# A new order for the first part of a one-core kernel: gated convolution, attention and channel mixing in one program

## The chip, the core and the metric

One core of a Trainium2 chip runs the whole program. The metric is the device time of one execution in microseconds (us), the median over runs. TensorE (PE) multiplies matrices; PEld is its weight load, which overlaps the multiplication. VectorE (DVE), ScalarE (ACT) and GpSimd (POOL) do elementwise work, and SyncE (SP) issues transfers. A row with a q behind the engine's name (SPq, ACTq) is a transfer being issued by that engine's queue.

## The reference

```python
kv = np.einsum('bhsd,bhse->bhde', k, v)            # q, k, v: (8, 8, 576, 64)
out = np.einsum('bhsd,bhde->bhse', q, kv)
out = out / np.sqrt(np.mean(out*out, -1, keepdims=True) + 1e-6) * g_norm
x = out.transpose(0, 2, 1, 3).reshape(8, 576, 512)

h = np.maximum(x @ w_in, 0.0)                      # w_in (512, 1024)
conv = sum(conv_w[j] * shift(h, j - 1) for j in range(3))   # along the sequence
x = (h / (1 + np.exp(-conv))) @ w_out              # w_out (1024, 512)

xn = (x - mean) / np.sqrt(var + 1e-6) * g_ln
out = x + np.maximum(xn @ w_ch1, 0.0) @ w_ch2      # (512, 2048), (2048, 512)
```

`shift` stands for the zero-padded copy of h moved by one row. The arithmetic is float32 (weights arrive as 64-bit numbers).

## The kernel before, in words

The 4608 rows of all batches are 36 tiles of 128 rows; three tiles make a chunk of 384 columns. The kernel is a list of small steps, each a Python function with arguments, and each has a place (a number, its slot). The list is sorted by place and written out in that order. Every engine runs its instructions strictly in the order in which they were written, and waits on semaphores for what it needs from the others. So the sorted list is the schedule: a step that waits holds up all later steps of its engine.

Names of steps, as they stand in the order (`b` a batch, `t` a tile of 128 rows, `f` one of 8 slices of w_in or w_out, `i` = 8 x chunk + f):

- `load_kvh_b_j`, `load_kvr_b`: k and v of a batch (two halves of 2 x 512 KB and a remainder of 2 x 128 KB); `load_q_t` (256 KB, tiles 0 to 3), `load_q2_u`: q of tiles 2u and 2u+1 in 16 or 32 small transfers; `load_w_winf`, `load_w_woutf` (512 KB each); `load_w_w10` is the first slice for the last part of the program. All transfers take one of 8 semaphores in turn, so the ninth waits for the first to land.
- Weights: `round_w0` (ACT, two instructions, L206 and L207), `cv_vec` (DVE, L213 and L214) and `cv_pool` (POOL, L221) turn the 64-bit number into float32. Then `split_win0`/`split_w0` (ACT, L248/L237) make the high half, `split_win1`/`split_w1` (DVE L253, or L242 on DVE or POOL) the low half, since each product is three passes of high and low halves.
- Attention: `kv_pair` (PE, L312), `kv_evac` (DVE, L319); `tq` and `tq_evac` (PE L360, ACT L365) transpose q for tiles 0 to 3, `tq_blocks` (DVE, L353) for later ones; `qkv` (PE, L377); `st_a`, `st_v`, `st_p` (ACT, DVE, POOL: the root mean square), `x_norm` (DVE, L404), `tx_first` (PE, L420), `xe_a`, `xe_l`, `xe_h` (ACT, DVE, POOL: the transposed tile and its low half, and the neighbours' columns).
- Convolution: `gemm1_i` (PE, L495, 12 matmuls into `h`), `conv_a` (ACT, L520), `conv_t` (first tap: L514 on DVE, L511 on ACT), `conv_v` (two taps on DVE, L535), `gate_a`, `gate_v` (ACT L546, DVE L552), `gsplit_a`, `gsplit_l` (ACT L556; low half L561 on POOL or DVE), `gemm2_c_f` (PE, L570, 9 matmuls into `accA`), `y_evac`, `y_store`.

The first chunk's `gemm1_0` needs tiles 0 to 3 and the first weight slice. Steps of the last part (names `w1`, `w2`, L580 and up) begin to mix in at slot 25.

Three tuples say which steps go to which engine: `TAP_VEC` (first taps on DVE), `LO_POOL` (low halves of w_out on POOL), `G_POOL` (low halves of the gate on POOL). The table `MOVED` gives single steps another place than the loops gave them:

```python
plan = [(slot + n * 1e-4, fn, args) for slot, evs in events.items() for n, (fn, args) in enumerate(evs)]
plan = [(MOVED.get(label(fn, args), pos), fn, args) for pos, fn, args in plan]
with tc.manual_schedule():
    for _, fn, args in sorted(plan, key=lambda e: e[0]):
        fn(*args)
```

Of the kernel before, what the change touches and what calls it, by code (L numbers as in the profile page):

```python
# [27 lines left out]

MOVED = {
# [28 lines left out]
G_POOL = tuple(range(21))  # L60


@with_exitstack
def tile_kernel(
# [949 lines left out]
    for c in range(CB):  # L1014
# [75 lines left out]
    def label(fn, args):  # L1090
        keys = ["".join(map(str, a)) if isinstance(a, tuple) else str(a) for a in args if isinstance(a, (int, str, tuple))]
        return "_".join([fn.__name__, *keys])

    plan = [(slot + n * 1e-4, fn, args) for slot, evs in events.items() for n, (fn, args) in enumerate(evs)]
    plan = [(MOVED.get(label(fn, args), pos), fn, args) for pos, fn, args in plan]
    with tc.manual_schedule():
        for _, fn, args in sorted(plan, key=lambda e: e[0]):
            fn(*args)
# [24 lines left out]
```

## Time and profile before

| | us |
|---|---|
| median of 3 runs | 1326.61 (1326.54 to 1329.29) |
| the profiled execution, its own time | 1328.66 |
| its span, first to last instruction | 1326.9 |
| PE busy in the span | 1274.0 (96%) |
| DVE, ACT, POOL busy | 910.1, 548.8, 284.8 |

PE is busy for 96% of the span, so what can be had lies in the 4% in which it is not, and in the stretches in which its clock is granted at less than full speed (a mean granted clock of 0.985). Busy shares over the whole span hide that the first 170 us look quite different from the rest; the rows below are therefore by stretch.

### The profile page before, as it was taken

What the parts mean: (1) busy time and instruction counts of PE and PEld (TensorE: products, weight loads), DVE (VectorE), ACT (ScalarE), POOL (GpSimd) and SP (SyncE); (2) the same over time, 40 slices, a digit from 0 to 9 for tenths busy, and PEclk for the clock granted to TensorE, in tenths of its full rate; (3) what the DMA queues carried; (4) which work ended last, traced back from release to release, by engine and by line L of the source; (5) the groups of instructions that cost most, each with busy time, mean ns of one, the idle gap of its engine ahead of it and who ended that gap; (6) DMA issues with size and microseconds to landing.
All of it is one profiled execution on the core that took longest, in us unless ns stands there. A gap on an engine that the chain in (4) does not pass through costs nothing.

```text
span 1326.9 us, 19380 instructions
## 1 busy us (share of the span) xinstructions
PE 1274.0 (96%) x6949; PEld 1136.9 (86%) x6949; DVE 910.1 (69%) x1752; ACT 548.8 (41%) x1063; POOL 284.8 (21%) x303
## 2 busy tenths in 40 slices
PE   6779999999999999999999999999999999999998
PEld 6668788989898989788888999899998999989997
DVE  3998787878888887777767666667666666673223
ACT  2664465556565566644442223222322322232221
POOL 2584443323333231133310000100000000100000
PEclk8799999999999999999999999999999999999999
DMA  9555267336552331487767674866576576656561
GB/s 279 137 139 126 67 183 200 112 82 187 157 152 73 100 116 45 154 283 254 259 243 293 193 244 151 300 207 208 192 271 203 176 277 231 209 205 258 174 222 48
DMA packets 184052, 245.90 MB, mean 185 GB/s; under 512 B 92668, under 2 KB 121364, under 8 KB 183956
## 3 DMA queue, kind: packets, MB, share of 16 engines
q1 hardware_dynamic: 182032, 243.59, 57.2%
q10 hardware_dynamic: 1924, 1.07, 0.3%
q8 instruction: 55, 0.90, 0.3%
q14 instruction: 41, 0.34, 0.1%
HBM read 202.66 MB, written 41.94 MB: 184 GB/s over the span
## 4 chain that ended last, share of the span: by engine, by line
PE 60%; DVE 17%; ACT 7%; SPq 6%; DMA 5%; issue 3%; POOL 1%; DVEq 0%; ACTq 0%; POOLq 0%
PE accB L814 27%; PE u L736 14%; PE v L736 7%; DVE a L535 5%; SPq L344 4%; PE accA L570 4%; PE h L495 4%; PE c L736 4%; DVE a L552 2%; DVE zx L428 2%; DMA raw_w<-in_moe_w_ch 2%; DMA raw_win<-in_moe_w_in 1%; ACT a L511 1%; ACT a L546 1%; ACT g L556 1%
## 5 line engine op out<-in xcount | busy, mean ns | idle before, releaser
L814 PE MATMUL accB<-w2s,r 128*128 128x512 f32 x1440 | 376.1, 393 | 0.0
L814 PEld LDWEIGHTS accB<-w2s,r 128*128 128x128 f32 x1440 | 267.3, 188 | 38.5
L736 PE MATMUL u<-z,w1s 128*128 128x384 f32 x1152 | 236.5, 340 | 8.2 <-DVE r L796 5.6
L495 PE MATMUL h<-xt,win 128*128 128x386 f32 (+1 forms) x1152 | 227.1, 346 | 6.6 <-ACT hs L520 3.4
L570 PE MATMUL accA<-wout,g 128*128 128x512 f32 x864 | 223.3, 402 | 8.4 <-DVE wout L242 2.6
L736 PEld LDWEIGHTS u<-z,w1s 128*128 128x128 f32 x1152 | 207.8, 189 | 27.4 <-DVE r L796 8.5
L495 PEld LDWEIGHTS h<-xt,win 128*128 128x128 f32 x1152 | 206.0, 191 | 15.8 <-ACT hs L520 4.8
L570 PEld LDWEIGHTS accA<-wout,g 128*128 128x128 f32 x864 | 160.2, 191 | 41.2 <-DVE wout L242 2.9
L791 ACT ACTIVATE r<-t 128x384 fp32r<-128x384 f32 x144 | 75.7, 526 | 261.6 <-DVE t L784 261.6
L778 ACT COPY u<-u 128x384 f32<-128x384 f32 x144 | 68.7, 477 | 218.5 <-PE u L736 218.5
L535 DVE SCALAR_TENSOR_TENSOR a<-hs,cols,a 128x384 f32<-128x384 f32 x192 | 138.9, 724 | 27.0 <-ACT a L511 23.1
L428 DVE STREAM_TRANSPOSE zx<-xc 32x128 f32<-32x128 f32 x480 | 145.3, 303 | 7.4
L796 DVE SCALAR_TENSOR_TENSOR r<-t,r 128x384 fp32r<-128x384 f32 x144 | 80.4, 559 | 85.2 <-ACT r L791 85.2
L679 POOL TENSOR_SCALAR mv<-mv 128x1 f32<-128x1 f32 x36 | 25.0, 694 | 478.8 <-DVE mv L670 470.9
L736 PE MATMUL v<-z,w1s 128*128 128x384 f32 x576 | 116.8, 337 | 0.0
L736 PEld LDWEIGHTS v<-z,w1s 128*128 128x128 f32 x576 | 103.6, 188 | 8.1
L784 DVE TENSOR_TENSOR t<-v,u 128x384 f32<-128x384 f32 x96 | 53.4, 556 | 73.7 <-ACT u L778 55.5
L546 ACT ACTIVATE a<-a 128x384 f32<-128x384 f32 x96 | 50.4, 525 | 116.0 <-DVE a L535 116.0
L400 POOL TENSOR_TENSOR r<-ss,mhalf 128x8 f32<-128x8 f32 x36 | 66.6, 1850 | 79.0 <-DVE ss L395 74.1
L221 POOL TENSOR_TENSOR cvw<-cvw,rnw 128x512 int32<-128x512 int32 x32 | 43.1, 1347 | 163.1 <-DVE cvw L214 118.0
L814 PE MATMUL accB<-w,r 128*128 128x512 f32 x288 | 76.6, 398 | 0.0
L556 ACT CAST g<-a 128x384 fp32r<-128x384 f32 x96 | 49.1, 512 | 66.3 <-DVE a L552 64.6
(106 smaller groups left out, 1408.5 us busy)
## 6 DMA issues: line engine op xcount, KB each, us to landing
w1s<-w_d SPq DMA_DIRECT2D x144, 512.0 KB, 5.3
w2s<-w_d SPq DMA_DIRECT2D x80, 512.0 KB, 5.3
raw_w<-in_moe_w_ch SPq DMA_DIRECT2D x32, 512.0 KB, 5.4
w_d<-w1f SPq DMA_DIRECT2D x24, 512.0 KB, 2.7
w1s<-w_d SPq DMA_DIRECT2D x48, 256.0 KB, 4.3
y_dr<-ya SPq DMA_DIRECT2D x36, 256.0 KB, 2.1
yb<-y_dr SPq DMA_DIRECT2D x36, 256.0 KB, 5.2
yr<-y_dr SPq DMA_DIRECT2D x36, 256.0 KB, 5.8
```

What stands on the lines that cost most here:

```text
L400: nc.gpsimd.tensor_tensor(out=r, in0=x_r[t], in1=mhalf, op=ALU.pow)
L428: nc.vector.transpose(out=out[32 * i : 32 * i + 32, :, a : a + 32], in_=src[a : a + 32, :, i, :])
L495: nc.tensor.matmul(ps[:, 0:n], lhsT=w[:, a, kk, :], rhs=x_t[c][b][:, kk, 0:n], start=(m == 0), stop=(m == 3 * KD - 1),)
L535: nc.vector.scalar_tensor_tensor(out=av, in0=segs(c, h, j), scalar=cols[:, j * FA + f : j * FA + f + 1], in1=av, op0=ALU.mult, op1=ALU.add,)
L546: nc.scalar.activation(out=a, in_=a, func=ACTF.Sigmoid)
L556: nc.scalar.copy(out=g[:, HI, :], in_=a_sb[i])
L570: nc.tensor.matmul(acc[c][r], lhsT=g[:, a, r * P : (r + 1) * P], rhs=w[:, b, :], start=(f == 0 and n == 0), stop=(f == FA - 1 and n == len ...
L736: nc.tensor.matmul(ps[:, 0:HT], lhsT=w[:, a, kk, :], rhs=z[b][:, kk, :], start=(start and n == 0), stop=(n == 5), skip_group_check=True,)
L778: nc.scalar.copy(out=t, in_=ch[c, p, "u"][:, 0:HT])
L791: nc.scalar.activation(out=g[:, HI, :], in_=cu[c, p, h], func=ACTF.Relu)
L796: engine.scalar_tensor_tensor(out=g[:, LO, :], in0=cu.pop((c, p, h)), scalar=0.0, in1=g[:, HI, :].bitcast(F32), op0=ALU.max, op1=ALU.subtract)
L814: nc.tensor.matmul(ch[c][r], lhsT=g[:, a, rr * P : (rr + 1) * P], rhs=w[:, b, :], start=(p == 0 and n < RB and m == 0), stop=(p == NPB - 1 ...
```

## The change

`MOVED` is replaced by two written-out orders. The first one names the steps in the order in which they stood; the second one, which overrides it, puts 354 steps (all up to slot 25) into another order, from the first load to `y_store_0`. Three tuples change: the first taps 0, 8, 11 and 12 go from DVE to ACT, the low halves of w_out slices 1, 2 and 7 go from POOL to DVE, and so do the gate's low halves 1, 8, 9 and 11.

```diff
-MOVED = {
-    "load_kvr_0": -100.95, "load_kvh_0_0": -100.9, "load_kvh_0_1": -100.8, "load_w_win0": -100.7, "load_w_win5": -99.8,
...
-TAP_VEC = (0, 1, 8, 9, 10, 11, 12, 13, 14)
-LO_POOL = (1, 2, 3, 4, 7)
-
-G_POOL = tuple(range(21))
+ORDERS = (
...
+    (-100.95, 25.0008, """
+        load_w_win0 load_q_1 load_kvh_0_0 load_kvr_0 load_kvh_0_1 load_q_0 load_w_win6 load_q_2 load_g load_consts load_q_3
...
+        gate_a_11 gate_v_11 gsplit_a_10 gsplit_l_10 tq_blocks_10 gsplit_a_11 gsplit_l_11 load_w_w10 gemm1_12 conv_a_12
+        conv_t_12 conv_v_12 gemm2_1_1 xe_h_8 load_q2_6 y_store_0
+"""),
+)
+TAP_VEC = (1, 9, 10, 13, 14)
+LO_POOL = (3, 4)
+
+G_POOL = (0, 2, 3, 4, 5, 6, 7, 10, 12, 13, 14, 15, 16, 17, 18, 19, 20)
...
-    plan = [(MOVED.get(label(fn, args), pos), fn, args) for pos, fn, args in plan]
+    placed = {}
+    for lo, hi, order in ORDERS:
+        names = order.split()
+        placed.update((name, lo + (hi - lo) * n / len(names)) for n, name in enumerate(names))
+    plan = [(placed.get(label(fn, args), pos), fn, args) for pos, fn, args in plan]
```

Before the change `load_w_w10` stood after `load_q2_6`, and `y_store_0` ahead of both.

ACT's first work after its loads, before the change (`win0` is the split of the first weight slice and needs g, `tq` to `qt` is the transposed q of tiles 1 and 0, `xn` the square of tile 0's product):

```order
L206 ACTIVATE cvwin_229<-raw_win_166 128x512
L207 ACTIVATE rnwin_230<-raw_win_166 128x512
L248 ACTIVATE win_283<-cvwin_229,g_100 128x512
L365 COPY qt_292<-tq_278 128x512
L365 COPY qt_294<-tq_287 128x512
L389 ACTIVATE xn_306<-x_296 128x512
```

And the same place after it:

```order
L253 ACTIVATE cvwin_184<-raw_win_154 128x512
L254 ACTIVATE rnwin_185<-raw_win_154 128x512
L412 COPY qt_288<-tq_283 128x512
L412 COPY qt_295<-tq_278 128x512
L436 ACTIVATE xn_297<-x_290 128x512
L295 ACTIVATE win_309<-cvwin_184,g_100 128x512
```

The split stands behind the two copies and the first square now. DVE around the first low halves of w_out, before (`a1`, `a2` are convolution items 1 and 2, `qt4`, `qt5` the transposed q of tiles 4 and 5):

```order
L319 COPY kvbd1_103<-kv1_508 64x4x64 x2
L242 TENSOR_TENSOR wout0_628<-cvwout0_574,wout0_628 128x512
L552 TENSOR_TENSOR a1_594<-hs1_592,a1_594 128x384
L213 TENSOR_SCALAR raw_win5_227<-cvwin5_630 128x512
L214 SCALAR_TENSOR_TENSOR cvwin5_630<-cvwin5_630,raw_win5_227 128x512
L353 STREAM_TRANSPOSE qt4_639<-q2_2_430 128x512
L353 STREAM_TRANSPOSE qt5_655<-q2_2_430 128x512
L535 SCALAR_TENSOR_TENSOR a2_662<-hs2_660,cols_99,a2_662 128x384 x2
```

And after:

```order
L260 TENSOR_SCALAR raw_win5_215<-cvwin5_621 128x512
L261 SCALAR_TENSOR_TENSOR cvwin5_621<-cvwin5_621,raw_win5_215 128x512
L289 TENSOR_TENSOR wout0_579<-cvwout0_511,wout0_579 128x512
L400 STREAM_TRANSPOSE qt4_644<-q2_2_421 128x512
L400 STREAM_TRANSPOSE qt5_647<-q2_2_421 128x512
L289 TENSOR_TENSOR wout1_653<-cvwout1_607,wout1_653 128x512
L608 TENSOR_TENSOR g1_659<-a1_574,g1_659 128x384
L582 SCALAR_TENSOR_TENSOR a2_657<-hs2_655,cols_99,a2_657 128x384 x2
```

The low halves of w_out slice 1 and of gate item 1 (`wout1`, `g1`) stand ahead of item 2's taps; they were POOL's. PE at the end of chunk 0, before (`kv2` is batch 2's k and v, of which `kvr2` is the remainder, `h11` is gemm1_11, `x8` is qkv_8, `accA0` with `wout6` and `wout7` are gemm2_0_6 and gemm2_0_7):

```order
L312 MATMUL kv2_1154<-vm2_0_500,kl2_0_498 64x64 x8
L312 MATMUL kv2_1154<-kvr2_999 64x64 x2
L495 MATMUL h11_1165<-xt1_0_412,win3_590 128x388
...
L377 MATMUL x8_1178<-kvbd1_103,qt8_1139 128x128 x4
L570 MATMUL accA0_0_689<-wout6_1050,g6_1044 128x512 x3
...
L312 MATMUL kv2_1154<-vm2_0_500,kl2_0_498 64x64 x8
L312 MATMUL kv2_1154<-kvr2_999 64x64 x2
L570 MATMUL accA0_0_689<-wout7_1147,g7_1090 128x512 x3
```

And after:

```order
L617 MATMUL accA0_0_816<-wout6_1000,g6_1091 128x512 x3
...
L424 MATMUL x8_1161<-kvbd1_103,qt8_1107 128x128 x4
L542 MATMUL h11_1166<-xt1_0_416,win3_577 128x388
...
L617 MATMUL accA0_0_816<-wout7_1184,g7_1103 128x512 x3
...
L359 MATMUL kv2_1204<-vm2_0_651,kl2_0_649 64x64 x8
L359 MATMUL kv2_1204<-kvr2_952 64x64 x2
```

All four pairs of batch 2 stand behind gemm2_0_7 now; the first of them stood ahead of gemm1_11.

## Rows read from the trace of the kernel before

**Rows 1.** Windows over the whole span: length, busy time of each engine, granted clock, transfers

```profile
0.00:41.40 41.40, 25.49 (x209) 22.83 (x209) 17.79 (x32) 14.92 (x28) 13.84 (x24) 0.79 0.94 250
41.40:95.30 53.90, 41.82 (x255) 35.65 (x255) 51.23 (x72) 33.59 (x64) 37.42 (x33) 0.91 0.56 146
95.30:121.70 26.40, 23.87 (x184) 21.11 (x183) 22.15 (x34) 12.16 (x25) 13.35 (x13) 0.94 0.55 137
121.70:150.00 28.30, 28.30 (x157) 25.93 (x156) 20.51 (x33) 12.07 (x25) 10.27 (x10) 1.00 0.39 87
150.00:170.00 20.00, 16.95 (x148) 13.29 (x147) 16.62 (x25) 11.33 (x24) 11.45 (x9) 1.00 0.24 93
170.00:1326.90 1156.90, 1137.58 (x6006) 1018.08 (x6005) 781.85 (x1559) 464.77 (x901) 198.51 (x218) 1.00 0.58 190
```

**Rows 2.** Timeline of the head: start, length, engine, work, idle time before and its releaser

```profile
12.81 0.34 PE L312 MATMUL kv<-kvr 128*64 128x64 f32 x4 [3.15 <-issue]
...
15.90 1.56 PE L360 MATMUL tq<-ident,q 128*128 128x128 f32 x8
...
19.34 0.15 DVE L164 TENSOR_SCALAR g<-g 128x1 f32<-128x1 f32 x1 [1.26 <-DMA g<-in_g_norm]
...
19.57 0.72 ACT L248 ACTIVATE win<-cvwin,g 128x512 fp32r<-128x512 f32 x1 [2.69 <-DVE g L164]
20.20 1.05 ACT L365 COPY qt<-tq 128x512 f32<-128x512 f32 x2
...
21.35 2.05 PE L377 MATMUL x<-kvbd,qt 128*128 128x128 f32 x8 [3.89 <-ACT qt L365]
...
41.38 3.64 PE L495 MATMUL h<-xt,win 128*128 128x386 f32 x12 [0.41 <-POOL xt L472]
```

**Rows 3.** Windows: the first 13.7 us; the last column is GB/s moved

```profile
0.00:13.70 13.70, 9.20 (x87) 8.97 (x89) 1.82 (x2) 1.49 (x2) 2.13 (x10) 0.99 0.96 228
```

**Rows 4.** Groups by line, 41.4 to 121.7: count, busy us, mean ns, idle before

```profile
L561 POOL TENSOR_TENSOR g<-a,g 128x384 fp32r<-128x384 f32 x11 | 13.0, 1188 | 6.1 <-ACT g L556 6.0
...
L242 POOL TENSOR_TENSOR wout<-cvwout,wout 128x512 fp32r<-128x512 f32 x5 | 7.5, 1507 | 2.8 <-ACT wout L237 2.8
...
L514 DVE TENSOR_SCALAR a<-hs,cols 128x384 f32<-128x384 f32 x5 | 5.8, 1170 | 0.4 <-POOL g L561 0.3
...
L242 DVE TENSOR_TENSOR wout<-cvwout,wout 128x512 fp32r<-128x512 f32 x3 | 3.1, 1031 | 0.0
```

**Rows 5.** The same view, 175 to 320 us: gate low halves on DVE

```profile
L561 DVE TENSOR_TENSOR g<-a,g 128x384 fp32r<-128x384 f32 x27 | 15.5, 574 | 7.6 <-ACT g L556 7.5
```

**Rows 6.** Timeline: a DVE conversion beside POOL, one alone, a tap alone

```profile
43.89 1.46 POOL L221 TENSOR_TENSOR cvwin<-cvwin,rnwin 128x512 int32<-128x512 int32 x1 [2.18 <-DVE rows L183]
44.24 1.66 DVE L214 SCALAR_TENSOR_TENSOR cvwin<-cvwin,raw_win 128x512 int32<-128x512 int32 x1
...
49.17 0.69 DVE L214 SCALAR_TENSOR_TENSOR cvwout<-cvwout,raw_wout 128x512 int32<-128x512 int32 x1
...
107.25 0.38 DVE L514 TENSOR_SCALAR a<-hs,cols 128x384 f32<-128x384 f32 x1
```

**Rows 7.** Timeline of PE at the end of chunk 0

```profile
102.07 2.35 PE L495 MATMUL h<-xt,win 128*128 128x388 f32 x12
...
107.57 0.34 PE L312 MATMUL kv<-kvr 128*64 128x64 f32 x4 [2.53 <-DMA kvr<-in_v]
107.83 3.26 PE L495 MATMUL h<-xt,win 128*128 128x388 f32 x12
```

**Rows 8.** Timeline, 121 to 165 us: SP's queue, ACT and PE

```profile
121.21 16.53 SPq L344 DMA_DIRECT2D q<-in_q  x32
137.79 0.98 SPq L228 DMA_DIRECT2D raw_w<-in_moe_w_ch  x2
...
164.62 1.66 PE L570 MATMUL accA<-wout,g 128*128 128x512 f32 x6 [2.00 <-ACT ya L580]
```

**Rows 9.** Who waited for whom, 120 to 172 us: total, times, longest

```profile
ACT cvw L206 <- DMA raw_w<-in_moe_w_ch: 2.9, 1, 2.9
```

More of the change, by code (lines that the diff above doesn't have):

```diff
@@ L27 @@
 REBIAS = 2.0**-112
-MOVED = {
[23 rows of a table removed]
-TAP_VEC = (0, 1, 8, 9, 10, 11, 12, 13, 14)
-LO_POOL = (1, 2, 3, 4, 7)
-G_POOL = tuple(range(21))
+ORDERS = (
+    (-100.95, 23.0007, """
+        load_kvr_0 load_kvh_0_0 load_kvh_0_1 load_w_win0 warm_22 load_g load_q_0 load_q_1 load_q_2 load_q_3 load_w_win1
+        load_consts load_w_win2 load_w_win3 load_w_wout0 load_kvh_1_0 load_kvr_1 load_kvh_1_1 load_w_win4 load_w_wout1
+        load_w_win5 round_w0_win0 cv_vec_win0 cv_pool_win0 kv_pair_0_0 kv_pair_0_1 kv_pair_0_2 kv_pair_0_3 scale_g tq_1
+        split_win0_0 kv_evac_0 tq_0 tq_evac_1 tq_evac_0 qkv_0 tq_2 st_a_0 st_v_0 st_p_0 qkv_1 st_a_1 st_v_1 st_p_1 x_norm_0
+        tq_3 tq_evac_2 qkv_2 st_a_2 st_v_2 st_p_2 x_norm_1 tx_first_0 tq_evac_3 qkv_3 st_a_3 round_w0_win1 split_win1_0
+        st_v_3 cv_vec_win1 st_p_3 xe_a_0 xe_l_0 round_w0_win2 xe_h_0 tx_first_1 x_norm_2 xe_a_1 x_norm_3 xe_l_1 cv_vec_win2
+        xe_h_1 cv_pool_win1 tx_first_2 xe_a_2 tx_first_3 split_win0_1 consts0 split_win1_1 xe_a_3 xe_l_3 consts1
+        cv_pool_win2 xe_l_2 split_win0_2 split_win1_2 consts2 xe_h_3 xe_h_2 load_q2_2 load_w_wout2 load_w_win6 load_w_wout3
+        load_w_win7 load_w_wout4 load_q2_3 load_w_wout6 load_w_wout5 load_kvh_2_1 load_kvh_2_0 load_w_wout7 round_w0_win4
+        kv_pair_1_0 round_w0_win3 cv_vec_win3 cv_pool_win3 gemm1_0 consts3 consts4 gemm1_1 kv_pair_1_1 conv_a_0 cv_vec_win4
+        consts5 conv_t_0 conv_v_0 round_w0_wout0 cv_vec_wout0 kv_pair_1_2 split_win0_3 conv_a_1 split_win1_3 conv_t_1
+        conv_v_1 gate_a_0 gate_v_0 cv_pool_win4 cv_pool_wout0 kv_pair_1_3 round_w0_wout1 split_win0_4 cv_vec_wout1
+        split_win1_4 gate_a_1 kv_evac_1 gsplit_a_0 gsplit_l_0 split_w0_wout0 round_w0_win5 split_w1_wout0 gate_v_1
+        cv_vec_win5 cv_pool_wout1 tq_blocks_4 cv_pool_win5 gemm1_2 tq_blocks_5 gsplit_a_1 gsplit_l_1 conv_a_2 conv_t_2
+        conv_v_2 split_w0_wout1 split_w1_wout1 round_w0_wout2 cv_vec_wout2 cv_pool_wout2 gemm1_3 gemm2_0_0 qkv_4 gate_a_2
+        gate_v_2 load_q2_4 st_a_4 st_v_4 st_p_4 split_win0_5 split_win1_5 round_w0_win6 cv_vec_win6 cv_pool_win6 x_norm_4
+        gsplit_a_2 conv_a_3 conv_t_3 split_w0_wout2 split_w1_wout2 qkv_5 st_a_5 round_w0_wout3 conv_v_3 gsplit_l_2 st_v_5
+        st_p_5 cv_vec_wout3 gate_a_3 gate_v_3 split_win0_6 split_win1_6 round_w0_win7 cv_vec_win7 gemm1_4 gemm1_5 tx_first_4
+        xe_a_4 x_norm_5 gsplit_a_3 cv_pool_wout3 cv_pool_win7 conv_a_4 conv_t_4 split_w0_wout3 split_w1_wout3 round_w0_wout4
+        gemm2_0_1 tq_blocks_6 conv_v_4 gemm1_6 qkv_6 xe_l_4 xe_h_4 st_a_6 conv_a_5 gate_a_4 split_win0_7 tx_first_5
+        gsplit_l_3 conv_t_5 round_w0_wout5 cv_vec_wout4 st_v_6 split_win1_7 gate_v_4 cv_pool_wout4 st_p_6 gsplit_a_4
+        gsplit_l_4 conv_v_5 split_w0_wout4 split_w1_wout4 cv_vec_wout5 gemm2_0_2 round_w0_wout6 conv_a_6 x_norm_6
+        cv_vec_wout6 cv_pool_wout5 xe_a_5 xe_l_5 xe_h_5 gate_a_5 gate_v_5 gemm2_0_3 gemm1_7 tx_first_6 xe_a_6 load_q2_5
+        conv_t_6 load_kvr_2 tq_blocks_7 gsplit_a_5 xe_l_6 conv_v_6 split_w0_wout5 split_w1_wout5 cv_pool_wout6 xe_h_6
+        gate_a_6 gemm2_0_4 qkv_7 st_a_7 conv_a_7 conv_t_7 st_v_7 gate_v_6 gsplit_l_5 gsplit_a_6 st_p_7 conv_v_7
+        split_w0_wout6 split_w1_wout6 round_w0_wout7 x_norm_7 cv_vec_wout7 gate_a_7 gate_v_7 gemm1_8 conv_a_8 load_kvh_3_0
+        load_kvr_3 load_kvh_3_1 gsplit_a_7 gsplit_l_6 conv_t_8 conv_v_8 gemm2_0_5 gemm1_9 tx_first_7 gemm1_10 conv_a_9
+        tq_blocks_8 gate_a_8 conv_t_9 xe_a_7 cv_pool_wout7 gsplit_l_7 gate_v_8 split_w0_wout7 xe_l_7 xe_h_7 gsplit_a_8
+        conv_v_9 kv_pair_2_0 gemm1_11 qkv_8 gemm2_0_6 tq_blocks_9 st_a_8 st_v_8 split_w1_wout7 st_p_8 gate_a_9 gate_v_9
+        kv_pair_2_1 gsplit_l_8 x_norm_8 gsplit_a_9 gsplit_l_9 conv_a_10 conv_t_10 conv_v_10 gemm2_0_7 kv_pair_2_2 y_evac_0_0
+        y_evac_0_1 y_evac_0_2 gate_a_10 gate_v_10 kv_pair_2_3 tx_first_8 y_store_0 kv_evac_2 gsplit_a_10 gsplit_l_10
+        conv_a_11 conv_t_11 conv_v_11 gemm2_1_0
@@ L63, in tile_kernel @@
+"""),
+)
+TAP_VEC = (1, 9, 10, 13, 14)
+LO_POOL = (3, 4)
+G_POOL = (0, 2, 3, 4, 5, 6, 7, 10, 12, 13, 14, 15, 16, 17, 18, 19, 20)
 @with_exitstack
```

30 lines of the change are left out of this document (added), and 22 rows, old and new, of the table MOVED.

## The prediction, made before the changed kernel ran

> **What bounds the kernel now.** I read the busy time by stretch first, because the shares over the whole span say only that PE is the bound. The windows [rows 1] show five stages. Until 41.4 us PE is idle for 15.9 us of 41.4 and its clock is granted at 0.79: the head, a chain of loads and small steps. From 41.4 to 95.3 DVE is busy for 51.2 of 53.9 us and PE for 41.8: DVE sets the pace, and PE loses 12.1 us in idling, and more at a clock of 0.91. From 95.3 to 121.7 PE is busy for 23.9 of 26.4 us, so PE is the bound again, but for one hole. From 121.7 to 150 PE is full. From 150 to 170 it idles for 3.05 us, and after that for 19.3 us of 1157, which the change doesn't touch. So at most 15.9 + 12.1 + 2.5 + 3.05 = 33.5 us of idle PE time, and what the lower clock costs, are within the change's reach.
>
> Then I read the timeline of each stage for what ends its waits. In the head, the last transposition of q ends at 15.90 + 1.56 = 17.46, but its copy on ACT starts at 20.20, because ACT stands at the split of the first weight slice, which waits for g until 19.57; so the first attention product starts at 21.35 [rows 2]. The first convolution matmul starts 20.0 us later, at 41.38, released by the last of a chain over four tiles [rows 2]. In the third stage the hole is a wait of 2.53 us for the remainder of batch 2's k and v, after which the 12 matmuls of a convolution item take 3.26 us instead of 2.35 [rows 7]. In the fifth, PE waits 2.00 us for a copy of its accumulator by ACT [rows 8]; ACT itself had waited 2.9 us for the first slice of w_ch1 [rows 9], which was issued at 137.79 behind 32 small transfers that take SP from 121.21 [rows 8].
>
> **The change part by part.**
>
> *Head.* The split moves behind the two copies. Then the copy of tile 0 can start at 17.46 and takes half of 1.05 us, and the product starts at about 18.05 if k and v of batch 0 are there as before: 21.35 - 18.05 = 3.3 us. Are they? Before, the remainder had landed by 12.81 [rows 2]. The new order puts slice 0 of w_in and tile 1 of q ahead of or between them: 2.25 MiB of k and v, 0.5 of weights and 0.25 of q are 3.0 MiB, 3.15 MB. The first 13.7 us moved 13.7 x 228 GB/s = 3.12 MB [rows 3], so they are complete near 13.8, one microsecond later. Two of the four pairs don't need the last block and can go before it. The other two, at about 1 us each (the last three took from 12.81 to 15.90 [rows 2]), end at 15.8, as before. If all four had to wait, they would end 1.1 us later. The head gains 2.2 to 3.3 us; I take 3.0, since the chain of 20.0 us behind it keeps its steps and changes their order a little. So the first convolution matmul should start at 38.4.
>
> *Second stage, DVE.* Moved onto DVE before the end of this stage are the low halves of w_out slices 1 and 2 and of gate item 1; moved off is tap 0. By the groups' means that is 2 x 1.03 + 0.57 - 1.17 = +1.5 us [rows 4, 5], and +2.3 if the tap would have met no POOL instruction and taken 0.38 us [rows 6]. POOL gets rid of three large instructions of 1.2 to 1.5 us [rows 4]. What that returns is not in one row: a conversion of 0.69 us took 1.66 us when it began 0.35 us after a POOL instruction of 1.46 us, 0.97 more [rows 6]. One that meets none loses nothing, so the three return 0 to 2.9 us; I take 2.0, two meetings of three. The Trainium skill states a rule for this (SBUF — State Buffer, section "Who interferes with whom"): a DVE instruction with two SBUF inputs and a GpSimd instruction that reads SBUF exclude each other, and the second waits for the first to end. The pair of rows agrees: POOL ended at 45.35, and DVE 0.55 us after that. By the rule the three could return up to their whole length, 4.2 us, which would make the time 2.2 us less than my sum; it also says that a low half on DVE still excludes POOL, which has idle time to give.
>
> New waits come in. Tap 0 goes to ACT, and it needs the constants whose transposition stands behind the first convolution matmuls, so DVE waits for these 3.64 us [rows 2], then for the transposition, a copy and the tap. With DVE 3 us early but these matmuls no faster, it may idle for nothing, if the conversions written ahead of the tap fill the time, or for as long as these matmuls take, 3.6 us. I take the middle, near which the conversions of slices 3 and 4 would bring it: +1.9 us. The stage in sum: +1.5 - 2.0 + 1.9 = 1.4 us of the lead is lost, 1.6 us is left. The loads I cost at nothing: the groups shown have no idle time that a transfer ended [rows 4], the transfers are the same ones in another order, and the one that comes much earlier (w_in 6, 0.52 MB) makes those behind it 2.3 us later by the rate above. If a conversion came to wait for them, that would be its price.
>
> *Third stage, PE.* All of batch 2's pairs move behind the last accumulation of chunk 0. Ahead of the first one there now stand item 11 (2.35 us [rows 7]) and, besides, a product and two accumulations; that alone is nearly the length of the hole of 2.53 us, and with the others more than PE's lead, so the hole is covered. With it goes the lower clock: 0.06 of 26.4 us is 1.6 us [rows 1]. Together -4.1 us. In exchange the low half of w_out slice 7 goes from POOL to DVE, where it stands behind both taps of item 9 and the square sums of tile 8, and PE's gemm2_0_7 needs it, with all four pairs and the next item's matmuls queued behind on PE. From tile 8's product on, PE has 2.35 us of item 11 to do, while ACT's square, DVE's sums and a low half of 1.03 us [rows 4] follow each other, and DVE may be late itself. I put a wait of 1.5 us there, between 0 and 4.1 (then the new hole is worth the old one). The stage gives -2.6 us.
>
> *Fifth stage.* The slice of w_ch1 is issued ahead of the 32 small transfers instead of behind them, so it lands more than 16 us sooner and ACT's 2.9 us go. PE's idle time there is 3.05 us [rows 1], and its 2.00 us wait for ACT's copy [rows 8] comes four DVE and ACT steps later, each of which can take over as the last one. I take 1.3 us, between 0 and 3.05. The stores that now stand behind the small transfers free tiles that nobody needs before chunk 2.
>
> *Sum.* 1.6 + 2.6 + 1.3 = 5.5 us off the profiled execution's own time, 1328.66, which gives 1323.2; that execution is 2.05 us above the median of the runs, so the prediction stands at 1326.61 - 5.5 = **1321.1 us**. From 170 us on PE is busy for 1137.6 of 1156.9 us and nothing is reordered, so a lead once won should stay.
>
> **The rivals.**
>
> *The lead is absorbed.* DVE could set the pace as before. If the three freed POOL instructions return nothing, the tap was worth 0.38 us and the new waits cost 3.6, the second stage takes 2.3 + 3.6 = 5.9 us, 2.9 more than the head gains. Then the end of chunk 0 moves by +2.9 - 2.6, and with nothing in the fifth stage the time is 1326.9. For it: DVE is busy for 95% of that stage [rows 1], and the change gives it more work. Against it: a POOL instruction does lengthen what it meets [rows 6].
>
> *Slower: DVE comes late to w_out slice 7.* By then DVE has taken over three low halves of w_out and two of the gate, 3 x 1.03 + 2 x 0.57 = 4.2 us [rows 4, 5], and given up two taps, 0.8 us at the least [rows 6]. If POOL's part returns nothing and the new waits are 3.6 us, DVE is 3.4 + 3.6 - 3.0 = 4.0 us later than before. PE then waits at gemm2_0_7 for this, for the 1.5 us that it waits there anyway, and loses 1.6 us to the lower clock behind the hole, as behind the old one: 7.1 us against the 4.1 that go. That is +3.0 us, 1329.6. It decides from a wait of some 4 us at that place on.
>
> *More: every hole closes.* With 3.3 us in the head, 2.9 returned, no new waits beyond 1 us, no wait at slice 7 and the fifth stage's 3.05: 3.3 - 1.5 + 2.9 - 1.0 + 4.1 + 3.05 = 10.85 us, 1315.8. For it: PE's 12.1 us of idle time in the second stage are there to be used, and the new order puts convolution matmuls ahead of accumulations. Against it: each term must come out at its best end.
>
> **How the numbers follow.** The forecast (3 to 8 us less) gets 0.50, the absorbed lead 0.21, the late slice 7 0.13, every hole closed 0.16. 0.2% is 2.65 us, about what a measurement of this kernel can tell from no change. Faster by more: 0.50 + 0.16 = 0.66; within: 0.21; slower: 0.13. The range reaches from 1313.5, a little below the last rival, to 1327.5, past the absorbed lead; outside it lie most of the late slice and a tail of the best case, 0.16.
>
> **What would show it.** In the changed profile: the first attention product near 18.0 and the first convolution matmul near 38.4; POOL's group of w_out low halves at 2 instead of 5 and DVE's at 6, with shorter means for DVE's conversions; no wait of PE for `kvr`; at the end of chunk 0 a wait of PE for DVE's `wout` of 1 to 2 us; ACT's wait for w_ch1 gone, and PE idle for less than 2 us between 150 and 170. The prediction is wrong if the first product starts after 20 us (then the loads were late), if DVE shows new waits of over 4 us in the second stage, or if PE loses its lead again after 170 us.

## The result and the profile after

The changed kernel takes 1315.97 us (median of 6 runs, 1314.11 to 1317.29) against 1329.12 us for the kernel before on the same chip (6 runs, 1326.54 to 1329.67): a ratio of 0.9906, with an interval of 0.9893 to 0.9919, or 12.5 us less (10.8 to 14.2). The ratio is taken over all runs; the two medians alone are 13.2 us apart. The profiled execution has a span of 1314.7 us against 1326.9. The time lies inside the range, but more than twice the forecast 5.5 us was gained; the rival in which every hole closes (1315.8 us) is nearest to it.

The windows of the same stretches as [rows 1], after the change:

```profile
0.00:41.40 41.40, 26.70 (x231) 23.62 (x233) 20.59 (x38) 18.16 (x33) 17.43 (x28) 0.84 0.94 262
41.40:95.30 53.90, 43.17 (x265) 38.66 (x260) 48.12 (x77) 35.67 (x70) 33.82 (x28) 0.87 0.56 142
95.30:121.70 26.40, 26.17 (x205) 23.16 (x204) 22.38 (x38) 12.78 (x27) 9.42 (x7) 1.00 0.60 144
121.70:150.00 28.30, 28.30 (x191) 25.18 (x190) 24.09 (x36) 12.78 (x25) 13.91 (x13) 1.00 0.34 89
150.00:170.00 20.00, 19.04 (x139) 16.25 (x136) 13.97 (x24) 12.55 (x26) 11.32 (x10) 1.00 0.51 177
170.00:1314.70 1144.70, 1126.87 (x5938) 1008.70 (x5936) 773.29 (x1545) 458.81 (x889) 191.78 (x212) 0.99 0.58 190
```

The third stage lost its hole and its lower clock (26.17 us of PE work at 1.00, instead of 23.87 at 0.94), and the fifth two thirds of its idle time (0.96 instead of 3.05 us). In the second stage DVE's idle time rose from 2.7 to 5.8 us, while PE did a little more at a lower clock (0.87 instead of 0.91). From 170 us on PE idles for 17.8 us instead of 19.3: the lead is kept.

The head, to be held against [rows 2] (timeline):

```profile
12.88 0.38 PE L359 MATMUL kv<-kvr 128*64 128x64 f32 x4 [2.50 <-DMA kvr<-in_v]
...
16.39 1.10 PE L407 MATMUL tq<-ident,q 128*128 128x128 f32 x8
16.57 0.86 DVE L366 COPY kvbd<-kv 64x256 f32<-64x256 f32 x2 [1.87 <-PE kv L359]
17.46 0.15 DVE L211 TENSOR_SCALAR g<-g 128x1 f32<-128x1 f32 x1
17.53 1.07 ACT L412 COPY qt<-tq 128x512 f32<-128x512 f32 x2 [4.03 <-PE tq L407]
...
18.21 1.13 PE L424 MATMUL x<-kvbd,qt 128*128 128x128 f32 x8 [0.72 <-ACT qt L412]
...
35.55 0.69 PE L542 MATMUL h<-xt,win 128*128 128x386 f32 x1 [3.41 <-POOL xt L519]
```

The first product starts at 18.21 instead of 21.35, and neither the copies nor the split wait for g any more. To read the gain stage by stage one needs points at which PE has the same work behind it. Three starts of PE's convolution items (1, 8, 12) and one copy of ACT (item 16), first before:

```profile
45.12 1.16 PE L495 MATMUL h<-xt,win 128*128 128x386 f32 x5
...
95.29 0.97 PE L495 MATMUL h<-xt,win 128*128 128x388 f32 x4
...
121.66 1.59 PE L495 MATMUL h<-xt,win 128*128 128x388 f32 x8
...
150.14 0.49 ACT L520 ACTIVATE hs<-h 128x386 f32<-128x386 f32 x1
```

and after:

```profile
41.13 0.64 PE L359 MATMUL kv<-vm,kl 128*64 128x64 f32 x16
...
41.81 2.38 PE L542 MATMUL h<-xt,win 128*128 128x386 f32 x12
...
90.24 4.48 PE L542 MATMUL h<-xt,win 128*128 128x388 f32 x24
...
112.64 1.05 PE L424 MATMUL x<-kvbd,qt 128*128 128x128 f32 x8
113.44 2.38 PE L542 MATMUL h<-xt,win 128*128 128x388 f32 x12
...
138.29 0.49 ACT L567 ACTIVATE hs<-h 128x386 f32<-128x386 f32 x1
```

| point | before | after | lead, same work | of this stage | forecast |
|---|---|---|---|---|---|
| PE, item 1 | 45.12 | 41.81, one pair more done (0.68) | 4.0 | +4.0 | +3.0 |
| PE, item 8 | 95.29 | 90.24 | 5.05 | +1.0 | -1.4 |
| PE, item 12 | 121.66 | 113.44, tile 9's product more done (0.80) | 9.0 | +4.0 | +2.6 |
| ACT, item 16 | 150.14 | 138.29 | 11.85 | +2.8 | +1.3 |
| span | 1326.9 | 1314.7 | 12.2 | +0.4 | 0 |

In this pair of executions all four terms came out on their better side. The end of chunk 0, PE's timeline, as in [rows 7]:

```profile
102.69 2.36 PE L542 MATMUL h<-xt,win 128*128 128x388 f32 x12
...
105.52 2.12 PE L617 MATMUL accA<-wout,g 128*128 128x512 f32 x8 [0.23 <-DVE wout L289]
107.57 0.69 PE L359 MATMUL kv<-vm,kl 128*64 128x64 f32 x16
```

The feared wait for w_out slice 7 is there, but 0.23 us long. SP's queue, ACT and PE around the first slice of w_ch1, as in [rows 8]:

```profile
106.49 1.55 SPq L275 DMA_DIRECT2D raw_w<-in_moe_w_ch  x1
...
129.88 0.65 ACT L253 ACTIVATE cvw<-raw_w 128x512 f32<-128x512 f32 x1
...
152.78 1.66 PE L617 MATMUL accA<-wout,g 128*128 128x512 f32 x6 [0.73 <-ACT ya L627]
```

SP issues the slice at 106.49 instead of 137.79, ahead of the 32 small transfers. ACT converts it at 129.88 without waiting for it (it waited 2.9 us, [rows 9]), and PE's wait for `ya` is 0.73 us instead of 2.00. The groups by line from 41.4 to 121.7 us, as in [rows 4], the first row from before:

```profile
L214 DVE SCALAR_TENSOR_TENSOR cvwout<-cvwout,raw_wout 128x512 int32<-128x512 int32 x8 | 7.2, 900 | 0.3
...
L261 DVE SCALAR_TENSOR_TENSOR cvwout<-cvwout,raw_wout 128x512 int32<-128x512 int32 x8 | 7.2, 901 | 0.3
...
L289 DVE TENSOR_TENSOR wout<-cvwout,wout 128x512 fp32r<-128x512 f32 x6 | 4.9, 820 | 0.0
...
L289 POOL TENSOR_TENSOR wout<-cvwout,wout 128x512 fp32r<-128x512 f32 x2 | 2.9, 1464 | 1.5 <-ACT wout L284 1.5
...
L608 DVE TENSOR_TENSOR g<-a,g 128x384 fp32r<-128x384 f32 x4 | 2.4, 599 | 0.0
...
L561 DVE TENSOR_SCALAR a<-hs,cols 128x384 f32<-128x384 f32 x3 | 1.2, 410 | 0.0
```

POOL's group of w_out stands at 2 and DVE's at 6, as the change says. DVE's first taps take 410 ns instead of 1170, its low halves of w_out 820 instead of 1031. But one sign of the prediction failed: the conversions with two inputs, the 0.69 us of [rows 6], are no shorter in the mean (901 ns after, 900 before); only their halves with one input are (569 ns for w_out, 778 before). I counted the lengthening for all of DVE: each instruction between 41.4 and 121.7 us against the lower quartile of its own kind. Before, DVE took 19.0 us longer than that over 54.7 us of work; after, 10.7 us over 60.1 (more work, since the window reaches further into the program). Grouping the kinds otherwise moves these totals by about 1 us. Instructions that began beside no POOL instruction lost nothing, in either kernel. The new waits, of the second stage (who waited for whom: total, times, longest):

```profile
PE x L424 <- DVE qt L400: 5.8, 1, 5.8
PE x L424 <- DVE xn L451: 4.5, 1, 4.5
...
DVE qt L400 <- DMA q<-in_q: 1.4, 1, 1.4
```

### The profile page after: what moved, and what is told of

Its sections match the earlier page's. It is cut to its first block, busy times and chain, and to the rows that moved or that the text cites. A ratio compares the mean times of both kernels' runs of the same rounds, so it can differ in the third digit from the quotient of the medians.

```text
span 1314.7 us, 19363 instructions
## 1 busy us (share of the span) xinstructions
PE 1270.2 (97%) x6949; PEld 1135.6 (86%) x6949; DVE 902.5 (69%) x1755; ACT 550.8 (42%) x1067; POOL 277.7 (21%) x296
## 4 chain that ended last, share of the span: by engine, by line
PE 60%; DVE 19%; ACT 8%; SPq 5%; DMA 4%; issue 3%; POOL 1%; DVEq 0%; ACTq 0%; POOLq 0%
PE accB L861 27%; PE u L783 14%; PE v L783 7%; DVE a L582 6%; PE c L783 4%; PE accA L617 4%; SPq L391 4%; PE h L542 3%; DVE a L599 2%; DVE zx L475 2%; ACT a L558 1%; ACT g L603 1%; ACT a L593 1%; DVE g L608 1%; ACT hs L567 1%
## 5 line engine op out<-in xcount | busy, mean ns | idle before, releaser
L582 DVE SCALAR_TENSOR_TENSOR a<-hs,cols,a 128x384 f32<-128x384 f32 x192 | 137.2, 714 | 29.5 <-ACT a L558 25.5
L599 DVE TENSOR_TENSOR a<-hs,a 128x384 f32<-128x384 f32 x96 | 62.9, 655 | 19.1 <-ACT a L593 18.9
```

The costliest lines, as they stand in the source:

```text
L582: nc.vector.scalar_tensor_tensor(out=av, in0=segs(c, h, j), scalar=cols[:, j * FA + f : j * FA + f + 1], in1=av, op0=ALU.mult, op1=ALU.add,)
L599: nc.vector.tensor_tensor(out=av, in0=segs(c, h, 1), in1=av, op=ALU.mult)
```

## The experiments

Each kernel was timed against the kernel before on the same chip. The changed kernel's order without its three tuples, or the tuples without the order, are cuts of the change; the others move one or a few steps, in the kernel before or in the changed one. The table has the times, and from each profiled execution the first product and the first convolution matmul on PE, and ACT's copies of items 12, 16 and 24 (us from the start). Differences in us are the ratio's, times 1327. The last column says how far the profiled execution's own time lies above the median of its kernel.

| kernel | ratio (95%) | us | product | conv | 12 | 16 | 24 | profiled |
|---|---|---|---|---|---|---|---|---|
| before | 1 | | 21.35 | 41.38 | 125.8 | 150.1 | 191.3 | -0.5 |
| changed | 0.9906 (0.9893 to 0.9919) | -12.5 | 18.21 | 35.55 | 116.8 | 138.3 | 179.5 | +0.5 |
| 1 tuples alone | 0.9989 (0.998 to 0.9999) | -1.5 | 21.67 | 40.88 | 125.2 | 149.5 | 190.7 | +2.7 |
| 2 order alone | 0.9929 (0.9915 to 0.9943) | -9.4 | 19.95 | 37.20 | 119.0 | 141.0 | 182.2 | +0.9 |
| 3 new head, old rest | 0.9976 (0.9967 to 0.9985) | -3.2 | 21.45 | 41.95 | 123.3 | 147.5 | 188.7 | +0.7 |
| 4 old head, new rest | 0.9938 (0.9925 to 0.9951) | -8.2 | 21.21 | 41.41 | 120.8 | 142.4 | 183.6 | +1.7 |
| 5 changed, w_ch1 late | 0.9952 (0.994 to 0.9964) | -6.4 | 18.68 | 35.94 | 115.8 | 139.3 | 181.5 | -2.6 |
| 6 changed, k and v pair early | 0.9931 (0.9918 to 0.9944) | -9.2 | 18.80 | 36.15 | 116.3 | 137.8 | 179.0 | -0.8 |
| 7 changed, all of w_out on DVE | 0.9936 (0.9925 to 0.9948) | -8.5 | 19.51 | 36.77 | 118.7 | 140.2 | 181.4 | +0.5 |
| 8 changed, q of tiles 4, 5 early | 0.9969 (0.996 to 0.9978) | -4.1 | 19.29 | 36.64 | 124.2 | 145.7 | 187.0 | +1.5 |
| 9 before, split late | 1.0001 (0.9991 to 1.001) | +0.1 | 20.43 | 39.74 | 123.8 | 147.6 | 188.8 | -1.5 |
| 10 changed, split first | 0.9899 (0.9885 to 0.9914) | -13.4 | 18.67 | 36.01 | 115.7 | 137.2 | 178.4 | -0.5 |
| 11 before, w_ch1 early | 0.9972 (0.9962 to 0.9982) | -3.7 | 21.49 | 40.62 | 125.4 | 147.2 | 188.5 | +1.9 |
| 12 before, k and v pair late | 0.9992 (0.9983 to 1.0001) | -1.1 | 21.14 | 41.25 | 123.5 | 147.8 | 190.2 | +0.6 |

The kernel before, at 1328.66 us in its profile, is 1.2 to 1.7 us above its medians in the experiments' rounds (1326.94 to 1327.47). Executions of one kernel differ by 2 us and more, in part by the head: with the same steps up to the first convolution matmul, the first product starts anywhere from 18.21 (changed) to 21.45 (experiment 3). It follows the landing of batch 0's remainder, for which PE waits until 12.88 in the one and 15.08 in the other. With the old steps it stays between 21.14 and 21.67. So a table row says something of a stage by its differences from column to column, and of the whole by its ratio.

**1 and 2, tuples or order.** Experiment 1 is the changed kernel with the first of the two written orders only, which is the old one:

```diff
-    for lo, hi, order in ORDERS:
+    for lo, hi, order in ORDERS[:1]:
```

> The old order with the new engine tuples alone. Theory A (fewer large POOL instructions lengthen DVE's less, and that is most of what the second stage gained): 2 to 4 us faster than the kernel before, DVE's conversions of 0.69 us shorter in the mean than 0.90, convolution item 8 starting 2 to 4 us earlier than 95.3. Theory B (the order alone does it; the moved low halves only cost DVE time): 0 to 3 us slower than the kernel before, item 8 no earlier.

Experiment 2 has both orders and the old tuples:

```diff
-TAP_VEC = (1, 9, 10, 13, 14)
-LO_POOL = (3, 4)
-G_POOL = (0, 2, 3, 4, 5, 6, 7, 10, 12, 13, 14, 15, 16, 17, 18, 19, 20)
+TAP_VEC = (0, 1, 8, 9, 10, 11, 12, 13, 14)
+LO_POOL = (1, 2, 3, 4, 7)
+G_POOL = tuple(range(21))
```

> The new order with the old engine tuples. Theory A: loses 2 to 4 us of the change's 12, so 8 to 10 us faster than before, with DVE's conversions lengthened as before. Theory B: as fast as the change or faster, 12 us or more below the kernel before.

The order alone gives 9.4 us, the tuples alone 1.5, which lies between experiment 1's two theories (2 to 4 faster, 0 to 3 slower). By the count above, DVE's lengthening between 41.4 and 121.7 falls from 19.0 to 14.2 us with the tuples and to 14.3 with the order. Each takes nearly the same off, yet one gains six times as much; the order also moves the head, the pair and the load of w_ch1. Experiment 2's time is that of theory A. The conversions, from which theory A of experiment 1 expected its gain, keep their mean there (900 ns for w_out). The trace of experiment 1, one of its slowest executions (1327.89 us, with a median of 1325.23), shows one place where its lead goes (PE's timeline, the wait of [rows 7]):

```profile
107.92 0.34 PE L359 MATMUL kv<-kvr 128*64 128x64 f32 x4 [4.36 <-DMA kvr<-in_v]
```

PE came to this pair at 102.88 instead of 104.35. It waits 4.36 us instead of 2.53 for the remainder of batch 2, and the transfer ends no sooner than before. The lead of 1.5 us that had reached PE was lost there in this execution; no trace shows one of the faster executions.

**3 and 4, head or rest.** Both take the steps up to `gemm1_0` from one of the two orders and all others, in their sequence, from the other; experiment 3 has the old tuples too.

```diff
+    old, new = (order.split() for _, _, order in ORDERS)
+    head = new[: new.index("gemm1_0")]
+    names = head + [n for n in old if n not in head]
```

> The new order up to the first convolution matmuls (the changed program's first convolution matmul started at 35.6), the old order and the old tuples behind it. Theory A (a lead won in the head is kept, since DVE sets the pace behind it): 4 to 6 us faster than before, all of the head's lead. Rival (absorbed: the loads or DVE's waits behind the head take it back): less than 2 us faster, and item 8 within 2 us of 95.3.

```diff
+    head = old[: old.index("gemm1_0")]
+    names = head + [n for n in new if n not in head]
```

> The old order up to the first convolution matmuls, the new order and the new tuples behind it. If the parts add up (theory A): 6 to 8 us faster than before, the change's 12 less the head's 5. Rival (the new rest needs the new head's loads and conversions to be early): less than 4 us faster.

The two gains, 3.2 and 8.2, add up to 11.4, within the interval of the whole; the first lies between its two theories, the second just above theory A's 6 to 8. But the cut is not a clean one. In experiment 3 the first pair of batch 1 stands ahead of the first convolution matmul, as before, while its remainder is loaded later, as in the new order (PE's timeline):

```profile
41.54 0.48 PE L359 MATMUL kv<-kvr 128*64 128x64 f32 x4 [3.85 <-DMA kvr<-in_v]
```

The convolution starts behind it at 41.95, so in this execution the new head brings no lead to it. About half of the 6.4 us by which it is behind the changed kernel's 35.55 is the late first product (21.45); the other half lies between that product and the convolution, where this wait stands. The moves of the pair and of its load belong together. Where its 3.2 us come from instead (the copy of item 12 is 2.5 us early, with a clock at 1.00 in the third stage) was not settled.

**9 and 10, the head's cause.** The prediction put the head's gain on the place of the split. Experiment 9 moves the split alone, in the kernel before:

```diff
+    placed["split_win0_0"] = placed["tq_evac_0"] + 1e-4
```

> The kernel before, with one step moved: the split of the first weight slice behind the first two copies of transposed q. As I predicted the step: the first attention product at 18.05 instead of 21.35, 3.3 us faster in the head and 2 to 3 us faster in the end. Rival (the evacuation of k and v's product stands behind the scaling of g on DVE, and that waits for g until 19.3 as well): the product starts at 20.3, and the kernel is 1 us faster at the most.

Experiment 10 moves it back ahead of the copies in the changed kernel, and the scaling of g ahead of the copy of k and v's product:

```diff
+    placed["scale_g"] = placed["kv_evac_0"] - 1e-4
+    placed["split_win0_0"] = placed["tq_evac_0"] - 1e-4
```

> The changed kernel, with the split of the first weight slice ahead of the first copies of transposed q again, and the scaling of g ahead of the evacuation on DVE again. If the place of the split made the head's gain: the first product 0.7 to 3 us later than 18.2 and the kernel 1 to 3 us slower than the changed one. Rival (g lands at 14 now instead of 19.2, because its loads come ahead of the last loads of q, and nobody would wait for it in either order): the product within 0.3 us of 18.2, no change.

In experiment 9 the copy on ACT runs early (17.34), and the first product waits for DVE instead (timeline):

```profile
19.33 0.15 DVE L211 TENSOR_SCALAR g<-g 128x1 f32<-128x1 f32 x1 [1.52 <-DMA g<-in_g_norm]
19.43 0.86 DVE L366 COPY kvbd<-kv 64x256 f32<-64x256 f32 x2
...
20.43 1.32 PE L424 MATMUL x<-kvbd,qt 128*128 128x128 f32 x8 [2.38 <-DVE kvbd L366]
```

DVE's copy of kv stands behind its own use of g, as the rival said. The time does not change (-1.2 to +1.3 us), although the profiled execution is 2.5 us early at item 24; it is 1.5 us below its median, and that of the kernel before 1.3 us above the median of this round. In experiment 10 both users of g stand first again, and cost nothing, because g is there (timeline):

```profile
14.97 0.15 DVE L211 TENSOR_SCALAR g<-g 128x1 f32<-128x1 f32 x1
...
16.38 0.72 ACT L295 ACTIVATE win<-cvwin,g 128x512 fp32r<-128x512 f32 x1 [2.65 <-POOL cvwin L268]
```

The product starts at 18.67, 0.5 us after the changed kernel's (the rival said within 0.3) but within the spread of this head, and the time, 1314.09 us, is the lowest measured but can't be told from the changed kernel's. So with g early the places of both steps do not matter. By the semaphores that they wait for, the two halves of g were the 13th and 14th transfer of the program and are the 9th and 10th now, and with 8 semaphores taken in turn ACT can issue the first at 3.92 us instead of 12.80. This is not the place of `load_g` in the written order, where the two moved from 8th and 9th to 12th and 13th: the transfers around it, on SP's and ACT's queues, changed places. The early g is enough for the head's gain. Whether it is needed is open: the changed order also puts DVE's copy of kv ahead of the scaling of g (16.57 and 17.46 above), and no run has that move and the split's together with a late g. The prediction's number was right, and the cause that it named, the split's place, does not do it alone.

**12 and 6, the hole of batch 2's remainder.** Experiment 12 moves the first pair behind item 11, tile 8's product and `gemm2_0_6` in the kernel before; experiment 6 moves it to its old place in the changed one:

```diff
+    placed["kv_pair_2_0"] = placed["kv_pair_2_1"] - 1e-4
```

> The kernel before with one step moved: the first pair of batch 2's k and v stands directly ahead of the second one, so behind the convolution matmuls of item 11, the product of tile 8 and the accumulation of w_out slice 6. Theory A (the prediction's term): the wait of 2.53 us for the remainder is covered, the clock does not fall behind it, and nothing else comes late; the matmuls of item 11 start at once behind item 10, and the time falls by 2.5 to 4.1 us, ratio 0.997 to 0.998. Theory B (DVE sets the pace of this stage too): item 11, tile 8's product or slice 6 then waits for DVE or ACT in place of the transfer, the time falls by less than 1 us, ratio above 0.9992, and the hole was worth next to nothing by itself. Theory C (the remainder's transfer is what counts, wherever the pair stands): the pair waits at its new place as well, since it lands at 107.6.

```diff
+    placed["kv_pair_2_0"] = placed["gemm1_11"] - 1e-4
```

> The changed kernel, with the first pair of batch 2 ahead of convolution item 11 again. Theory A (the hole was the remainder's landing, and its place in the order alone hides it): the remainder lands near 103, the pair comes near 102.7, so 0 to 1.5 us slower than the changed kernel with a wait of that length. Rival (the transfers of q come earlier too, so it has long landed): 0, and no wait at that place.

In experiment 12 the hole closes, the clock stays up, and item 12 starts 3.65 us earlier than before (118.01), as the prediction's term says. Then it is given back (PE, ACT and PE in one timeline; the last two waits are those of [rows 8, 9]):

```profile
118.01 2.27 PE L542 MATMUL h<-xt,win 128*128 128x388 f32 x12
...
139.74 0.67 ACT L253 ACTIVATE cvw<-raw_w 128x512 f32<-128x512 f32 x1 [2.75 <-DMA raw_w<-in_moe_w_ch]
...
148.30 2.39 PE L542 MATMUL h<-xt,win 128*128 128x386 f32 x12 [1.29 <-ACT hs L567]
...
162.22 3.54 PE L617 MATMUL accA<-wout,g 128*128 128x512 f32 x9 [2.00 <-ACT ya L627]
```

ACT still waits 2.75 us for w_ch1, PE waits 1.29 us more for ACT, and the clock falls to 0.91 between 150 and 170 us. Of 3.65 us, 2.4 are left at item 16, 1.1 at item 24, and 1.1 (-0.1 to 2.3) in the times. The trace is theory A's as far as item 12, the time near theory B's. In experiment 6 the old place costs a wait of 0.43 us:

```profile
102.97 0.34 PE L359 MATMUL kv<-kvr 128*64 128x64 f32 x4 [0.43 <-DMA kvr<-in_v]
```

The remainder is there at 102.97 instead of 107.57, as SP reaches it sooner, and the copies of items 12 to 24 come within 0.6 us of experiment 10's. By its ratio it is 3 us slower than the changed kernel, by its profile not slower at all; anything below 3 us is open here. The hole closes by the earlier transfer as well as by the later pair.

**11 and 5, the first slice of w_ch1.** Experiment 11 issues it ahead of `y_store_0` and the small transfers in the kernel before; experiment 5 puts both back as they stood, in the changed kernel:

```diff
+    placed["load_w_w10"] = placed["y_store_0"] - 1e-4
```

> The kernel before, with one step moved: the load of the first slice of w_ch1 ahead of the stores and the 32 small transfers of q. Theory A: ACT's wait of 2.9 us goes, PE's idle time between 150 and 170 falls from 3 to 1 us, the kernel is 1.3 to 3 us faster than before. Rival (the hole stays, since DVE's sums for w_ch1 stand in front of the copies): within 0.5 us.

```diff
+    placed["y_store_0"] = placed["load_w_w10"]
+    placed["load_w_w10"] = placed["load_q2_6"] + 1e-4
```

> The changed kernel, with the first slice of w_ch1 issued behind the 32 small transfers of q again and the stores ahead of both. Theory A (that slice's late landing holds ACT and costs PE the fifth stage's hole): 1.3 to 3 us slower than the changed kernel, ACT waits for the slice again, PE idle near 3 us where the changed kernel has 1. Rival (the hole of the fifth stage came from DVE's sums for w_ch1 and closes whatever the slice does): within 0.5 us of the changed kernel.

This one edit gives the kernel before 3.7 us (2.4 to 5.0), the most of any single one and above theory A's 1.3 to 3. SP issues the slice at 108.61 instead of 137.79, ACT doesn't wait, and of PE's 3.05 idle us between 150 and 170 only 1.3 are left (windows of experiment 11):

```profile
150.00:170.00 20.00, 18.74 (x160) 15.64 (x159) 16.62 (x25) 10.95 (x22) 11.47 (x9) 1.00 0.24 93
```

Experiment 5 takes the same away again: ACT's wait is back at 2.36 us, PE's for `ya` at 2.0, and the clock falls to 0.91. Against experiment 6, which ran beside it with the same head, it is 3.0 us slower by the medians (1319.73 and 1316.71) and 2.5 us late at item 24. Against the changed kernel its ratio makes it 6 us slower, more than theory A's 1.3 to 3, and nothing here says where the rest would come from.

**7 and 8, further in the same direction.** Experiment 7 moves the last two low halves of w_out from POOL to DVE; experiment 8 loads q of tiles 4 and 5 ahead of batch 1's k and v, since the changed kernel's longest wait on PE is for these tiles:

```diff
-LO_POOL = (3, 4)
+LO_POOL = ()
```

> The changed kernel, with the low halves of w_out slices 3 and 4 on DVE as well, so none on POOL. Theory A (what POOL gives back is worth more than what DVE takes on): 0 to 1.5 us faster than the changed kernel. Theory B (DVE's work is what counts): 1 to 2 us slower, two times 0.7 us.

```diff
+    placed["load_w_wout0"] = placed["load_w_wout1"] + 1e-4
+    placed["load_q2_2"] = placed["load_w_wout1"] + 2e-4
+    for j in range(4):
+        placed[f"kv_pair_1_{j}"] = placed["gemm1_2"] + (j + 1) * 1e-4
+    placed["kv_evac_1"] = placed["tq_blocks_4"] - 1e-4
```

> The changed kernel, with the small transfers of q for tiles 4 and 5 issued ahead of batch 1's k and v instead of behind them, and batch 1's pairs behind convolution item 2. In the changed kernel DVE waits 1.4 us for these transfers at 53 and PE 5.8 us for DVE behind that. Theory A (in the second stage DVE's time is what counts): 1 to 2 us faster than the changed kernel. Rival (PE's idle time there is refilled later, or batch 1's pairs come too late): no change, or slower by 1 to 3 us.

Neither helps. Experiment 7 is 4.0 us slower than the changed kernel by the ratios and 1.3 us slower than experiment 6 by the medians, where theory B said 1 to 2. Its DVE's lengthening falls once more, to 8.6 us, but DVE now waits for ACT's half of w_out, and PE for DVE (waits, 41.4 to 95.3 us):

```profile
PE x L424 <- DVE xn L451: 7.8, 1, 7.8
...
DVE wout L289 <- ACT wout L284: 2.7, 2, 2.1
```

In experiment 8 PE waits for batch 1's k and v instead of for q (timeline), twice as long, and the time is 5.9 us above experiment 6's, more than the rival's 1 to 3:

```profile
50.83 0.89 PE L359 MATMUL kv<-vm,kl 128*64 128x64 f32 x16 [4.95 <-DMA vm<-in_v]
57.71 0.48 PE L359 MATMUL kv<-kvr 128*64 128x64 f32 x4 [6.00 <-DMA kvr<-in_v]
```

## Why the prediction was right in its direction and short in its size

**Head: +4.0 at equal work, against +3.0.** The first product was forecast for 18.05 and came at 18.21, and k and v of batch 0 were there in time, as worked out. The step that failed is the cause given, that the split moves behind the copies: by experiment 9 the wait for g stood on DVE too, ahead of the copy of kv, and by experiment 10 the split's place costs nothing once g is early. I had not priced g's earlier load, nor the move of DVE's copy. That the number came within 0.2 us is in part luck: in the other kernels with this head the product starts 0.5 to 3.2 us later. The extra microsecond is in the sentence that the chain of 20.0 us "keeps its steps": it became 17.34 (18.21 to 35.55). In part this is PE's clock, which before was granted at 0.50 from 21.0 to 25.6 us, behind the wait of 3.89 us, and at 1.00 from 18 to 22 us after. The first 8 matmuls of the product took 2.05 us before ([rows 2]) and 1.13 after. Batch 1's first pair was not in the way: behind it PE still waited 0.41 us for POOL's edge columns ([rows 2]). The forecast for the first convolution matmul, 38.4, was 2.9 us late.

**Second stage: +1.0, against -1.4.** The work that was moved was priced nearly rightly: by the means after the change it is 2 x 0.82 + 0.60 - 1.17 = 1.1 us instead of 1.5. What POOL's relief returns was not. I gave it 2.0 us, for three instructions less, and took the price from a conversion, whose mean did not change. The tuples alone, as far as the end of the third stage, take 4.8 us off DVE's lengthening, the order alone 4.7, both 8.3. I had reckoned only with the number of POOL's instructions; which of DVE's instructions stand beside them is worth as much. Against that, DVE's idle time rose by 3.1 us, where I took 1.9, and "the loads I cost at nothing" failed for one: q of tiles 4 and 5 kept DVE waiting for 1.4 us in the profiled execution (it did not in experiment 10). The price named there, "if a conversion came to wait for them", was the right kind of price for another step. PE's waits for these tiles grew to 5.8 and 4.5 us, and still the lead grew across the stage: DVE, not PE, sets the pace there. In experiments 6 and 10, with the same steps in this stage, the first convolution matmul is 0.6 and 0.5 us later than in the changed kernel and ACT's copy of item 8 is 1.0 and 1.1 us earlier (92.01 and 91.88 against 93.02), so the +1.0 is a low reading of what the stage gives.

**Third stage: +4.0, against +2.6.** The hole and the lower clock went, as forecast at 4.1 us. The wait for w_out slice 7 was mis-sized: 0.23 us instead of 1.5.

**Fifth stage: +2.8, against +1.3.** The step was right, its size not: I let the four steps behind ACT take over half of its 2.9 us, and they took over almost nothing. Experiment 11 gives 3.7 us for it, experiment 5 2.5 to 3.0 against experiment 6.

**The sum.** The rival in which every hole closes (10.85 us) was nearest, and it got 0.16 because "each term must come out at its best end". That treats the terms as independent, and they are not. Alone, the tuples give 1.5 us and the pair's move 1.1; in their traces these leads run into the next landing that does not move: the remainder at 107.6 to 107.9, then w_ch1 at 139 to 142. (The split alone gives nothing in the times for another reason: with DVE's wait for g the product came 0.9 us earlier, not 3.3.) The change moves these landings too, so that a lead from one stage is not taken away in the next. The halves by which I cut the terms, for a wait that takes over, were prices of single edits. Experiments 1 and 12 show them for single edits; in the change they did not fall due. What is shown, in one execution each, is that these two leads were lost at these two places, the second not wholly. That nothing else is lost is read from the table of leads, also one execution of each kernel.

## What to carry to other kernels

Where a queue's transfers fix when a stage can begin, a lead won before it can be worth little until that landing moves too; cost a bundle of edits by the landings that remain, not by the sum of what each would give alone. The cheapest edit can be the place of one issue in a queue: one load put ahead of 32 small transfers and a store gave 3.7 us here, the whole reassignment of work between engines 1.5. And when a prediction's time is met, test its cause: here the first product came within 0.2 us of the forecast, while the step that the forecast named does not bring it there alone.

## What the hardware showed that I had not expected

A long POOL instruction need not lengthen DVE. The pair of [rows 6] is found again after the change, and again DVE's conversion ends 0.55 us after POOL's; but the same conversion beside POOL's power of 128x8 numbers, which takes 1.6 to 2.1 us, keeps its 0.69 us (timeline, both in the changed kernel):

```profile
51.09 1.31 POOL L268 TENSOR_TENSOR cvwout<-cvwout,rnwout 128x512 int32<-128x512 int32 x1 [1.62 <-DVE cvwout L261]
51.32 1.63 DVE L261 SCALAR_TENSOR_TENSOR cvwin<-cvwin,raw_win 128x512 int32<-128x512 int32 x1
...
61.55 2.07 POOL L447 TENSOR_TENSOR r<-ss,mhalf 128x8 f32<-128x8 f32 x1 [0.36 <-DVE ss L442]
62.51 0.69 DVE L261 SCALAR_TENSOR_TENSOR cvwin<-cvwin,raw_win 128x512 int32<-128x512 int32 x1
```

I went through every meeting of this kind before 125 us, in both kernels: no DVE instruction with two inputs that began beside POOL's power lost more than 0.1 us to it (13 such meetings before, 14 after). The prediction drew on the Trainium skill (SBUF — State Buffer, "Who interferes with whom"), by which such a pair exclude each other for the whole of the first instruction. The first pair of rows agrees with that, the second does not; the rows decide, and POOL's time by the profile is therefore no measure of what it costs DVE. A count of POOL's instructions, or of its busy time, misses this. An order that puts DVE's conversions beside the power could gain by it; no run tests that, and the two orders here have nearly the same number of such meetings.

Small transfers cost SP time by the piece, 0.5 to 0.65 us each in the mean of such a row: 48 take it 29.6 us before the change ([rows 8] show 32 in 16.53 us), 30.0 in experiment 1 and 30.7 after. Most follow each other every 0.47 us; the rest of the time SP waits, mostly for large transfers ahead to land. SP begins the 48 at 73.67 before and at 73.78 in experiment 1. That is why the remainder behind them lands at nearly the same time in the kernel before and in experiment 1, and a lead on the other engines waits for it.
